# A decay-delta recurrence with a conv-gate MoE: the state spread to a block diagonal by GpSimd, wide products, and a new order

## The chip, the cores and the metric

The kernel runs on one core of one Trainium2 chip. Five engines work beside each other, each through its own instructions in program order: TensorE (PE; its weight loads are counted apart as PEld), VectorE (DVE), ScalarE (ACT), GpSimd (POOL) and SyncE (SP), which issues the DMAs. The metric is the device time of one execution in microseconds. The kernel before takes 618.69 us, the median of three runs between 618.66 and 619.24.

## What is computed

Per batch element and head a 40x40 state runs through 768 positions. Its decay works on the columns, and it is read by r and by a, and added to by outer products of v and k and of the read by a with b. What comes out is a token's 320 values, which pass through a matrix, a convolution of three positions, a gate and a second matrix.

```python
batch, n_heads, seq, head_dim = (4, 8, 768, 40)
...
for t in range(S):
    y[:, :, t] = np.einsum('bhd,bhde->bhe', rt, state)
    Sa = np.einsum('bhde,bhe->bhd', state, at)
    state_decay = state * wt[:, :, None, :] - np.einsum('bhd,bhe->bhde', Sa, bt)
    state = state_decay + np.einsum('bhd,bhe->bhde', vt, kt)
...
h = np.maximum(x @ w_in, 0.0)                 # 320 -> 1024
conv_out += conv_w[k][None, None, :] * hp[:, k:k + S, :]   # 3 positions
gate = 1.0 / (1.0 + np.exp(-conv_out))
return (h * gate @ w_out).astype(np.float32)  # 1024 -> 320
```

## The kernel before

**Tiles.** The sequence is cut into 24 steps of 32 positions (C), n = 0 to 23, and two steps make a pair j. Within a step the recurrence is solved in blocks: decays are brought to the step's ends as running products, so that the work of 32 positions becomes matrix products and one triangular solve per pair. The eight heads stand in three groups (NH = 3, 3, 2) of up to 120 rows, 3 heads by 40. The state `s` is a tile of [120, 4 batch elements, 3 groups, 40]: the rows are three heads under each other, each with its 40x40 block.

**A step, by names.** `wakb` loads w, a, k and b. `decays` (L474 to L496) makes the running products and `wc`, the decay over a whole step for each row, batch element and group. `decayed` makes `ah`, a times its decay, and the same for k and b. `scores` (L541 to L561) makes `ap`, a copy of `ah` for each head in which the rows of the two other heads of the group are zero (three activations with the column of `hmask` as scale, L547), and from it and k, b the scores `at`. The solve of a pair (L598 to L633) runs on GpSimd in 15 small steps, cut in pieces at 4, 8 and 12 (`CUTS`), except that of pair 0 on VectorE, and its result goes through DRAM (`xd`, `tt`, `nb`). `chain` (L637 to L733) is the recurrence itself, in stages: `pp` takes the product of the state with `ap` (L645, 32 matmuls with 120 rows, 32 columns of weights and 40 columns moving, one for each head and batch element) and adds that of the scores with v (L656); `pw`, `pe` and `pu` apply the solve (L668, L679, L692) with `psb` and `w` between them; `vu` gets the solved rows; `pn` is the update of the state (L711), which VectorE adds to the old state in four instructions (L726); and GpSimd multiplies the new state by `wc` in place (L732), so that the next step finds it decayed. Because `ap` is zero outside its head, a product over all 120 rows gives the head's own rows alone.

**Outputs.** `pvt` turns `vu` (L764), `pt` the decayed state into `sn` (L774, L776), `pm` are the scores of r (L523), `py` the step's output (L798, L809). Two steps make a window of 64 positions, which goes through the MoE: `ph` (L861), the gate `cc` on VectorE (L890), and `po` (L906). In the opening the weights are loaded and converted in pieces (`wi02` is a piece of the first matrix; its two parts are `wih` and `wil`), by ACT (L300), VectorE and GpSimd (L315, L342).

**What sets the order.** Each piece of work is a generator, advanced to its next `yield` by a token of a long string, `ORDER`; `ch3` advances the chain of step 3, `we5` the weights of piece 5, `dd2.0` the `decayed` of pair 2. `put` names for each stage the stages that have to be emitted ahead of it, mostly because of the number of buffers (`BUFS`). Each engine runs its instructions in the order in which the tokens emit them.

Of the kernel before, what the change touches and what calls it, by code (L numbers as in the profile page):

```python
# [40 lines left out]
    ha2 dd0.1 ch0 ut0*2 dd2.0 ch0 so1 ld2 we4 we6 we7 pa0 we7 ou0 we6 we8 ou0 ha3 rt0 ch1 ha3 ou0
    lv2 dd2.0 we6 dd2.0 so1 si1 dd2.1 we8 we7 ch1 ld2 so1 ch1 st1 we7 sc4 dd2.1 fi0 we9 lv2 dd2.1
    ch1 we9 fi0 ch1 sc4 so0 ut1 we9*2 ch1 ut1 si0 ld3 we7 ha3 ld3 ch1 we8*2 ou1 we10 we11 lr1*2 we10
    fi0 ch0 so1 de3.0 sc5 pa1 ch2 we10 sc5 we11 we10 ou0 we12 lv3 ou1 ch2 ha2 lv3 we12 st2 we11 ch2
    rt1 we10 ch2 ut1 we11 we13*2 we0 fi1 si2 so2 ch2 rt1 we13 fi1 we12*2 we14 we12 dd1.0 we9 fi1 lr2
    si2 pa0 de3.0 we11 de3.0 ld3 we8 dd2.0 we14 ch2 we14 ha4 we13 we15 ut2 ou2 ut2 ch2 so2 we14 so2
    we16 pa2 ha4 so2 de3.1 dd3.0 we15 ou2 we15*2 we5 we17 ut0 ro0 ch3 de3.1 lv1 ha5 fi2 ha4 st3 ch3
    we16 ch3 ha5 ch3 we17 pa0 ld3 pk0 we17*2 ld3 we16 ut2 we16 we18 lv4*2 st1 dd3.0*2 pk0 dd3.0
    dd3.1*2 fi2 we16 ro0 st2 ch3 we19 mi0.0 dd3.1 ut3*2 lr2 ou3 ld4 fi2 we17 we18 ch0 ch3 pa3 ch3
    sc6 we18 we17 fi1 sc6 sc7 mi0.0 sc7 we19 sc6 mi0.0 we18 ha5 so2 rt2 ou3 de0.1 ut3 we20*2 mi0.0  # L50
    we19*2 ch4 we17 mi0.0 we20 de4.0 ha6 we20 ch2 de3.1 mi0.1 we18 ch4 lv5 we21 mi0.0 mi0.1 rt2 ch4
    we21 mi0.0 lr0 mi0.1 rt2 ld4 ch4 we22 lv5 we21 st4 ut0 fi3 ha6 ch4 de4.0 we22 mi0.2 we18 ut4 fi3
    we19 fi3 de4.1 we19 ld4 we20 ch4 we19 ut4 ch2 ou4 ch4 si3 so3 pa4 mi0.0 mi0.1 mi0.2 lv5 mi0.2
    si3 ou4 de4.1 ld4 we21 ou3 mi0.3 mi0.1*2 dd4.0 ha7 st2 ld5 mi0.1*2 mi0.3 mi0.1 ch5*2 mi0.3 st5
    ha7 lr3 dd4.0 ch5 mi0.2 dd4.0 dd4.1 so3 lv6 we20 so3 mi0.1 mi0.2 ou4 we18 mi0.0 dd4.1 ch5 pk1
    mi1.0 sc8 pk1 ch5 ld5 mi0.3 mi0.0 mi0.2 ou5 so3 lr3 mi0.2 fi4 de5.0 dd4.1 ut5*2 mi0.2 ha6 mi0.3
    ch5 pa5 mi1.0 we20 so3 mi1.0 ha7 ch5 dd4.0 fi4 mi0.3 mi1.1 ou5 fi4 sc8 sc9 ch2 lr3 st6 lr3 mi0.3
    fi5*2 mi1.0 ch5 de5.0 lv6 dd5.0 lv7 lv6 rt3 pa2 ut2 ch6*2 rt3 lv7 mi0.3 mi1.1 lv6 fi4 mi1.1 lr4
    de5.0 mi1.2 lv5 fi5 ch6 lv1 sc9 ch6 mi1.1 mo0.0 ld5 mi1.0 rt3 mi1.1 ha8 lv8 ch6 ha8 mo0.0 lv7
    mi0.2 mi1.1 ut6*2 dd4.1 ou6 mi1.0*2 fi0 lv7 mi1.1 pa6 lr2 ch5 ch6 ou6 de2.0 fi3 mi1.0 mi1.1  # L60
    mi0.3 mo0.0 mi1.0 mo0.0 ha9 ha8 mi1.2 de5.1 lr4 ha9 ld5 mi0.3 si4 dd5.0 mi1.0 fi4 mi0.2 ld5 ch6
# [1086 lines left out]
```

## Time and profile before

| what | us |
|---|---|
| median of 3 runs | 618.69 |
| the profiled execution | 619.69 |
| its span, first to last instruction | 617.1 |
| the chain's products with the state, pp<-s,ap (L645) on PE | 19.2 busy |
| the state times its decay on POOL (L732) | 24.3 busy |
| the masked a, ap (L547) on ACT | 36.3 busy |
| weight loads of pp, one group of rows (L645) | 106 to 118 ns each |

The profile is of one execution. Busy time counts what an engine works on; several instructions of an engine may run beside each other on PE, where the four 32-column quarters of the array take separate products, so that PE's mean duration of one matmul is longer than the distance of their starts. In rows of matmuls, "120*32" is the rows and columns of the weights, "120x40" the rows and columns that move, and each matmul in these 32-bit numbers leaves two records. Releasers ("<-") are inferred.

### The profile page before, as it was taken

The numbers are of one execution on the slowest core, as the hardware profiler recorded it, in microseconds if no ns is written. First come the engines' busy times: TensorE is split into PE (matmuls) and PEld (weight loads), VectorE is DVE, ScalarE is ACT, GpSimd is POOL, SyncE is SP. The second block draws the span as 40 slices with busy tenths as digits, with TensorE's granted clock in tenths as the row PEclk, the third lists the DMA queues.
The fourth block names the chain that finished last, engine by engine and source line by source line (L and its number), as shares of the span: only waits on it lengthen the run. The fifth ranks groups of instructions, "written<-read, shape, count | busy, mean of one in ns | idle before, by whom it ended". The sixth has DMA issues, their size and how long they took to land.

```text
span 617.1 us, 32909 instructions
## 1 busy us (share of the span) xinstructions
PE 540.9 (88%) x14861; PEld 454.1 (74%) x14861; DVE 371.1 (60%) x757; ACT 349.2 (57%) x852; POOL 238.7 (39%) x573
## 2 busy tenths in 40 slices
PE   4465788879989999899899899889999899989998
PEld 3355667768868888778788788678787786877884
DVE  7887677778756645656467554447664473434560
ACT  2444455575765647656667466366765474555551
POOL 3414766625725435236145444045346054020100
PEclk9856987799999999999999999899999999899999
DMA  9966837375264561711735426424431302101001
GB/s 149 141 119 130 149 94 160 79 159 94 39 133 77 101 109 17 140 34 25 136 68 96 92 51 102 97 55 70 102 56 33 86 13 51 36 4 29 17 20 35
DMA packets 214767, 49.32 MB, mean 80 GB/s; under 512 B 203324, under 2 KB 208404, under 8 KB 214628
## 3 DMA queue, kind: packets, MB, share of 16 engines
q1 hardware_dynamic: 214628, 47.23, 40.3%
q8 instruction: 116, 1.90, 1.3%
q14 instruction: 23, 0.19, 0.1%
HBM read 36.72 MB, written 9.18 MB: 74 GB/s over the span
## 4 chain that ended last, share of the span: by engine, by line
PE 75%; DVE 7%; issue 6%; DMA 5%; ACT 5%; POOL 0%; SPq 0%; DVEq 0%; ACTq 0%
PE po L906 16%; PE ph L861 15%; PE pm L523 4%; PE ps L523 3%; PE pe L679 3%; PE pn L711 3%; PE pu L692 3%; PE pw L668 3%; PE py L809 3%; PE pp L656 3%; PE pvt L764 2%; PE pz L568 2%; PE py L798 2%; PE pp L645 2%; DMA xh<-xh 2%
## 5 line engine op out<-in xcount | busy, mean ns | idle before, releaser
L906 PE MATMUL po<-wo,g 128*128 128x320 f32 x384 | 117.4, 443 | 3.8 <-issue 3.8
L890 DVE SCALAR_TENSOR_TENSOR cc<-hb,cw,cc 128x256 f32<-128x256 f32 x192 | 95.9, 521 | 30.7 <-ACT cc L882 27.1
L906 PEld LDWEIGHTS po<-wo,g 128*128 128x128 f32 x384 | 69.2, 193 | 26.3 <-issue 4.8
L732 POOL TENSOR_TENSOR s<-s,wc 120x480 f32<-120x480 f32 x23 | 24.3, 1058 | 109.1 <-DVE s L726 89.4
L611 POOL TENSOR_TENSOR stg<-xx,bb 128x15 f32<-128x15 f32 (+4 forms) x165 | 54.9, 333 | 29.4 <-DMA bb<-bd 17.7
L617 POOL TENSOR_TENSOR xx<-xx,stg 128x15 f32<-128x15 f32 (+4 forms) x165 | 56.6, 343 | 12.9
L699 ACT COPY vu<-pu 32x320 f32<-32x320 f32 x96 | 40.0, 417 | 33.0 <-PE pu L692 31.2
L861 PE MATMUL ph<-xh,wih 120*128 120x256 f32 x288 | 56.8, 305 | 1.1 <-DMA xh<-xh 1.1
L726 DVE SCALAR_TENSOR_TENSOR s<-pn,side,s 120x240 f32<-120x240 f32 x90 | 35.9, 461 | 28.2 <-PE pn L711 28.2
L898 DVE TENSOR_TENSOR g<-cc,hb 128x512 f32<-128x512 f32 x48 | 36.5, 765 | 23.5 <-ACT cc L895 23.3
L837 POOL TENSOR_TENSOR xl<-xf,xh 120x384 fp32r<-120x384 f32 x24 | 25.4, 1057 | 59.6 <-ACT xh L835 59.6
L875 ACT ACTIVATE hb<-ph 128x512 f32<-128x512 f32 x48 | 28.6, 597 | 32.7 <-PE ph L861 28.9
L861 PEld LDWEIGHTS ph<-xh,wih 120*128 120x128 f32 x288 | 41.4, 192 | 4.7 <-DMA xh<-xh 1.5
L882 ACT ACTIVATE cc<-hb,cw 128x256 f32<-128x256 f32 x96 | 43.5, 507 | 0.0
L425 POOL COPY vu<-vin 96x240 f32<-96x240 f32 (+1 forms) x72 | 28.0, 425 | 37.0 <-DMA vin<-in_v_dram 24.7
L749 ACT ACTIVATE rp<-pr,hmask 120x384 f32<-120x384 f32 (+1 forms) x72 | 34.0, 551 | 12.3 <-PE pr L747 9.4
L683 DVE SCALAR_TENSOR_TENSOR psb<-pe,half,psb 128x320 f32<-128x320 f32 x24 | 13.2, 551 | 45.4 <-PE pe L679 44.9
L547 ACT ACTIVATE ap<-ah,hmask 120x384 f32<-120x384 f32 (+1 forms) x72 | 36.3, 573 | 7.0 <-DVE ah L502 6.9
L861 PE MATMUL ph<-xh,wil 120*128 120x256 f32 x192 | 38.9, 283 | 0.3
L523 PE MATMUL ps<-ap,kt 120*64 120x96 f32 (+1 forms) x576 | 31.0, 264 | 8.6 <-DVE wi01q L305 5.3
L861 PE MATMUL ph<-xl,wih 120*128 120x256 f32 x192 | 38.5, 282 | 0.0
L895 ACT ACTIVATE cc<-cc 128x512 f32<-128x512 f32 x48 | 30.2, 634 | 11.7 <-DVE cc L890 11.6
(306 smaller groups left out, 1179.2 us busy)
## 6 DMA issues: line engine op xcount, KB each, us to landing
inw<-in_w_dram SPq DMA_DIRECT2D x24, 160.0 KB
ina<-in_a_dram SPq DMA_DIRECT2D x24, 160.0 KB
ink<-in_k_dram SPq DMA_DIRECT2D x24, 160.0 KB
inb<-in_b_dram SPq DMA_DIRECT2D x24, 160.0 KB
vin<-in_v_dram SPq DMA_DIRECT2D x48, 80.0 KB
rin<-in_r_dram SPq DMA_DIRECT2D x24, 160.0 KB
out_dram<-ob SPq DMA_DIRECT2D x22, 160.0 KB
bd<-at SPq DMA_DIRECT2D x24, 128.0 KB
```

Source lines behind the costliest of these rows:

```text
L523: nc.tensor.matmul(ps[hs, y, pick(g), :], lhs(g, y)[:, hs], mk(pick(g), z, y), start=(g == 0 and y == 0), stop=True, skip_group_check=True,)
L547: nc.scalar.activation(out=ap[:, by_set(h)], in_=ah[:, : NH[h]], func=AF.Copy, scale=hmask[:, h : h + 1])
L611: eng.tensor_tensor(t3, xx[:, 0:nj, i : i + 1].to_broadcast([128, nj, nt]), bb[:, i : i + 1, i + 1 :].to_broadcast([128, nj, nt]), ALU.mult,)
L617: eng.tensor_tensor(xx[:, 0:nj, i + 1 :], xx[:, 0:nj, i + 1 :], t3, ALU.add)
L699: nc.scalar.copy(vu[q, y, :HD], pu[y][q])
L726: nc.vector.scalar_tensor_tensor(out=dst, in0=src, scalar=side[:, x : x + 1], in1=dst if x else old[:, zs], op0=ALU.mult, op1=ALU.add,)
L749: nc.scalar.activation(out=rp[:, by_rows(g), y], in_=pr[:GR, : NH[g]], func=AF.Copy, scale=hmask[:, g : g + 1],)
L861: nc.tensor.matmul(ph[:, j], l[:, fs], x, start=(j == 0 and i == 0), stop=(i == len(passes) - 1), skip_group_check=True,)
L882: nc.scalar.activation(out=cc[:, j], in_=hb[:, j, :, 1 : W + 1], func=AF.Copy, scale=cw[:, 1, f : f + 1],)
L890: nc.vector.scalar_tensor_tensor(out=cc[:, j], in0=hb[:, j, :, x : W + x], scalar=cw[:, x, f : f + 1], in1=cc[:, j], op0=ALU.mult, op1=ALU ...
L898: nc.vector.tensor_tensor(gt, cc, hb[:, :, :, 1 : W + 1], ALU.mult)
L906: nc.tensor.matmul(po[:rows, :DM], part(f), wo[:, f, :], start=(f == 0), stop=(f == NF - 1))
```

## The change

The first product of `chain` takes the unmasked `ah` as weights (32 columns: the positions), and what moves is no longer the state of one head but a tile `wide` (`se`, [120, 4, 3, 3, 40]): for each group, three blocks of 40 columns, the state with all rows but those of one head set to zero, a block diagonal. So one matmul with 120 columns covers three heads, one with 80 columns the two heads of the last group: 12 matmuls instead of 32. GpSimd makes `se` after the state's update, in three products of 120x480 with `ws`, ahead of the old product with `wc`, which stays for `pt` and the next update. `ws` is `wc` times `hmask`, made by GpSimd in `decays`, two small products a call. `ap` stays for the scores. `ah` now lives until the chain has used it, and has four buffers instead of two; `ap` has two instead of six, `ws` three and `se` one. `chain` takes `st["vu"]` a stage later. The string ORDER is another from its first line to its last.

```diff
--- before.py
+++ after.py
@@ -22,7 +22,7 @@
 VSOL = (0,)
 NWA = 24
 BUFS = dict(
-    rin=1, rs=1, vin=1, vu=2, hat=6, suf=2, pre=3, wc=3, at=3, ah=2, kt=1, ap=6, rp=1, bb=2, xx=2, stv=1, stg=1,
+    rin=1, rs=1, vin=1, vu=2, hat=6, suf=2, pre=3, wc=3, at=3, ah=4, kt=1, ap=2, ws=3, se=1, rp=1, bb=2, xx=2, stv=1, stg=1,
     tt=2, nb=2, s=2, psb=1, w1=1, vt=2, sn=2, g=6, ms=1, xf=1, xh=2, xl=2, hb=2, cc=2, o=2,
 )
 KINDS = dict(
@@ -33,116 +33,115 @@
 ORDER = """
-    ld0*2 de0.0*2 ld0 dd0.0 ld0 lv0 de0.1 we0 de0.1 dd0.0*3 de0.0 dd0.1*3 ld1 sc0 we1 ha0 we0 sc0
...
+    ld0*2 de0.0*2 ld0*3 de0.1 ld1 we0 lv0 dd0.0 de0.1 dd0.0*2 dd0.1*2 ha0 dd0.0 dd0.1 we1 sc0 lv0
...
 """
@@ -489,6 +488,18 @@
         al = pd["wc"].rearrange("p c (z y) g -> p y g z c", y=2)[:, y]
         nc.vector.tensor_tensor(al, ends(suf, 0), ends(wr, 1), ALU.mult)
         nc.vector.reciprocal(ends(dp0, 0), al)
+        if y == 0:
+            pd["ws"] = buf(wn, [GR, 2, B, G, 3], "ws", f"ws{j}")
+        nc.gpsimd.tensor_tensor(
+            pd["ws"].rearrange("p c (z y) g h -> p y c z g h", y=2)[:, y, 0],
+            pd["wc"].rearrange("p c (z y) g -> p y c z g", y=2)[:, y, 0].unsqueeze(3).to_broadcast([GR, 2, G, 3]),
+            hmask.unsqueeze(1).unsqueeze(1).to_broadcast([GR, 2, G, 3]), ALU.mult,
+        )
+        nc.gpsimd.tensor_tensor(
+            pd["ws"].rearrange("p c (z y) g h -> p y c z g h", y=2)[:, y, 1],
+            pd["wc"].rearrange("p c (z y) g -> p y c z g", y=2)[:, y, 1].unsqueeze(3).to_broadcast([GR, 2, G, 3]),
+            hmask.unsqueeze(1).unsqueeze(1).to_broadcast([GR, 2, G, 3]), ALU.mult,
+        )
         nc.vector.tensor_tensor_scan(
             out=flat(pd["pre"][:, y]), data0=flat(wr), data1=flat(dp0),
             initial=0.0, op0=ALU.mult, op1=ALU.add,
@@ -637,17 +648,19 @@
     def chain(st, nxt):
         n, c, pd = st["n"], st["c"], st["pd"]
         att = pd["at"]
-        first, old, vu = n == 0, state[n], st["vu"]
+        first, old = n == 0, state[n]
         pp = bank([128, HD], f"pp{n}")
         if not first:
-            for q, g, h in heads():
+            ah, wide = gbt(pd["ah"][:, c]), st["wide"]
+            for g in range(G):
                 for bi in range(B):
                     nc.tensor.matmul(
-                        pp[quad(bi), q * D : (q + 1) * D], st["ap"][:, q, quad(bi)],
-                        old[:, bi, g],
-                        start=(q == 0), stop=False, skip_group_check=True,
+                        pp[quad(bi), g * GR : g * GR + NH[g] * D], ah[:, g, quad(bi)],
+                        wide[:, bi, g, : NH[g]],
+                        start=(g == 0), stop=False, skip_group_check=True,
                     )
         yield
+        vu = st["vu"]
         for h in range(H):
             hc = slice(h * D, (h + 1) * D)
             for bi in range(B):
@@ -729,6 +742,14 @@
                     )
         yield
         w4 = nxt["pd"]["wc"][:, nxt["c"]].unsqueeze(3).to_broadcast([GR, B, G, D])
+        wide = nxt["wide"] = buf(wn, [GR, B, G, 3, D], "se", f"se{n}")
+        ws = nxt["pd"]["ws"][:, nxt["c"]].rearrange("p b g h -> p (b g) h")
+        for h in range(3):
+            nc.gpsimd.tensor_tensor(
+                wide.rearrange("p b g h d -> p (b g) h d")[:, :, h],
+                new.rearrange("p b g d -> p (b g) d"),
+                ws[:, :, h : h + 1].to_broadcast([GR, B * G, D]), ALU.mult,
+            )
         nc.gpsimd.tensor_tensor(new, new, w4, ALU.mult)
         yield

@@ -1018,7 +1039,7 @@
             put(
                 ("decayed", j, y), lambda pd=pd, y=y: decayed(pd, y),
                 (0, ("wakb", j), 2), (0, ("decays", j, y), 2), (0, ("decayed", j - 1 + y, 1 - y), 3),
-                (0, ("scores", 2 * (j - BUFS["ah"]) + 1), 1), (1, ("wakb", j), 3), (2, ("wakb", j), 4),
+                (0, ("chain", 2 * (j - BUFS["ah"]) + 1), 1), (1, ("wakb", j), 3), (2, ("wakb", j), 4),
                 (1, ("scores", n + 1 - 2 * BUFS["kt"]), 2), (1, ("hats", n + 1 - 2 * BUFS["kt"]), 2),
             )
         put(
@@ -1042,7 +1063,7 @@
         put(
             ("scores", n), lambda st=st: scores(st),
             (0, ("decayed", j, 1), 1), (0, ("scores", n - 1), 2), (1, ("decayed", j, 1), 3),
-            (1, ("chain", 2 * (j - BUFS["at"]) + 1), 2), (0, ("chain", n - BUFS["ap"]), 1),
+            (1, ("chain", 2 * (j - BUFS["at"]) + 1), 2), (0, ("scores", n - BUFS["ap"]), 2),
         )
         put(
             ("hats", n), lambda st=st: hats(st), (0, ("decayed", j, 1), 2), (1, ("decayed", j, 1), 3),
```

On PE, from the last matmul of step 10's state update (`pn101`) to the product of step 11 with the state (`pp11`). Before:

```order
L711 MATMUL pn101_5560<-vu0_142,hat101_4792 56x80
L764 MATMUL pvt101_5590<-ident_80,vu0_142 120x128 x3
L906 MATMUL po20_5535<-wo_154,g21_5157 128x320 x2
L798 MATMUL py10_5621<-sn10_5425,rp5_5339 32x40 x32
L523 MATMUL pm10_5655<-rp5_5339,vt100_5557 64x3x32 x2
L523 MATMUL pm10_5655<-rp5_5339,vt101_5594 64x3x32 x2
L523 MATMUL pm10_5655<-rp5_5339,vt100_5557 64x3x32 x2
L523 MATMUL pm10_5655<-rp5_5339,vt101_5594 64x3x32 x2
L523 MATMUL pm10_5655<-rp5_5339,vt100_5557 64x2x32 x2
L523 MATMUL pm10_5655<-rp5_5339,vt101_5594 64x2x32 x2
L645 MATMUL pp11_5671<-s10_5585,ap11_4304 32x40 x32
```

And now; `se10` is the spread state, and four matmuls of 80 columns follow the eight of 120:

```order
L785 MATMUL pvt100_5492<-ident_80,vu0_142 120x128 x3
L785 MATMUL pvt101_5498<-ident_80,vu0_142 120x128 x3
L927 MATMUL po20_5458<-wo_154,g21_4935 128x320 x2
L927 MATMUL po20_5458<-wo_154,g22_5311 128x320 x2
L534 MATMUL pm10_5508<-rp5_5202,vt100_5496 64x3x32 x2
L534 MATMUL pm10_5508<-rp5_5202,vt101_5502 64x3x32 x2
L534 MATMUL pm10_5508<-rp5_5202,vt100_5496 64x3x32 x2
L534 MATMUL pm10_5508<-rp5_5202,vt101_5502 64x3x32 x2
L534 MATMUL pm10_5508<-rp5_5202,vt100_5496 64x2x32 x2
L534 MATMUL pm10_5508<-rp5_5202,vt101_5502 64x2x32 x2
L819 MATMUL py10_5528<-sn10_5408,rp5_5202 32x40 x32
L657 MATMUL pp11_5564<-se10_5523,ah5_3431 32x120 x8
```

Between the two stand now both `pvt` and four matmuls of `po` instead of one `pvt` and two, and `py` has changed places with `pm`.

On POOL, in the solve of pair 1 (`xx1`, `stg1`) at the first state `s0`, before:

```order
L611 TENSOR_TENSOR stg1_3_710<-xx1_699,bb1_696 128x48
L617 TENSOR_TENSOR xx1_699<-xx1_699,stg1_3_710 128x4x12
L732 TENSOR_TENSOR s0_788<-s0_788,wc0_164 120x480
L611 TENSOR_TENSOR stg1_4_812<-xx1_699,bb1_696 128x55
L617 TENSOR_TENSOR xx1_699<-xx1_699,stg1_4_812 128x5x11
L611 TENSOR_TENSOR stg1_5_815<-xx1_699,bb1_696 128x60
```

And now, with a weight piece behind it:

```order
L622 TENSOR_TENSOR stg1_3_867<-xx1_856,bb1_651 128x48
L628 TENSOR_TENSOR xx1_856<-xx1_856,stg1_3_867 128x4x12
L748 TENSOR_TENSOR se0_885<-s0_773,ws0_175 120x12x40 x3
L753 TENSOR_TENSOR s0_773<-s0_773,wc0_164 120x480
L341 TENSOR_TENSOR wil_153<-wi11q_406,wih_152 120x256
L622 TENSOR_TENSOR stg1_4_943<-xx1_856,bb1_651 128x55
```

The spread of the state stands ahead of the product with `wc0`. Further on in the same solve, from its eighth step to its ninth, before:

```order
L611 TENSOR_TENSOR stg1_7_821<-xx1_699,bb1_696 128x64
L617 TENSOR_TENSOR xx1_699<-xx1_699,stg1_7_821 128x8x8
L315 TENSOR_TENSOR wi12q_828<-wi12q_828 120x256
L342 TENSOR_TENSOR wil_153<-wi02q_592,wih_152 120x256
L611 TENSOR_TENSOR stg1_8_948<-xx1_699,bb1_696 128x63
L617 TENSOR_TENSOR xx1_699<-xx1_699,stg1_8_948 128x9x7
```

And now:

```order
L622 TENSOR_TENSOR stg1_7_952<-xx1_856,bb1_651 128x64
L628 TENSOR_TENSOR xx1_856<-xx1_856,stg1_7_952 128x8x8
L314 TENSOR_TENSOR wi02q_939<-wi02q_939 120x256
L424 COPY vu0_142<-vin_136 96x2x120 x2
L424 COPY vu0_142<-vin_136 96x2x80
L341 TENSOR_TENSOR wil_153<-wi21q_587,wih_152 80x256
L314 TENSOR_TENSOR wi12q_972<-wi12q_972 120x256
L341 TENSOR_TENSOR wil_153<-wi02q_939,wih_152 120x256
L341 TENSOR_TENSOR wil_153<-wi12q_972,wih_152 120x256
L622 TENSOR_TENSOR stg1_8_1074<-xx1_856,bb1_651 128x63
L628 TENSOR_TENSOR xx1_856<-xx1_856,stg1_8_1074 128x9x7
```

The copies of v for step 2 (`vu0<-vin`) and more pieces of the first matrix (`wi`, `wil`) stand now inside the solve.

On ACT, around `w10`, the second stage of step 0's chain, before:

```order
L481 COPY wx0_148<-pw21_601 120x12x31
L482 COPY wx1_150<-pw21_601 120x12x31
L749 ACTIVATE rp0_434<-pr01_607,hmask_85 120x3x128 x2
L749 ACTIVATE rp0_434<-pr01_607,hmask_85 120x2x128
L300 ACTIVATE wi02q_592<-wi02r_591 120x256
L673 ACTIVATE w10_654<-pw0_621,half_105 128x320
L340 CAST wih_152<-wi21q_581 80x256
```

And now:

```order
L339 CAST wih_152<-wi01q_387 120x256
L480 COPY wx0_148<-pw20_565 120x12x31
L481 COPY wx1_150<-pw20_565 120x12x31
L686 ACTIVATE w10_624<-pw0_591,half_105 128x320
L581 COPY hat20_630<-pz20_626 128x360
L299 ACTIVATE wi21q_587<-wi21r_586 80x256
L480 COPY wx0_148<-pw21_654 120x12x31
```

`w10` stood behind the conversion of `wi02`; that conversion now comes sixteen instructions after it.

More of the change, by code (lines that the diff above doesn't have):

```diff
@@ L41 @@
[L41 to L61, printed above, removed]
@@ new lines @@
+    fi3 ch4 ha6 mi0.1 de3.0 mi0.2 we20 we22 ch4 fi3 ch4 mi0.1 st4 ut4*2 ou4 pa4 ou4 mi0.0 lv6 dd4.0
+    de4.1 ch5 so3 de4.1 so1 ch5 mi0.2*2 mi0.3 ha7 so3 ch5 mi0.1 pa4 ha7 dd4.0 mi0.1 ch5 st5 ld4 ha7
+    dd4.0 mi0.2 so3*2 st1 ld5 mi0.1 mi0.3 lr1 de4.0 mi0.2 si3 mi0.1 mi0.3 ch5 mi0.2 dd4.1 pk1
+    dd4.1*2 ut5 sc8 we21 fi4 mi0.2 ut5 de5.0 ch5 mi1.0 mi0.2 ou5 ld5 mi1.0 mi0.3 pa5 sc8 sc9 sc8 ou5
+    mi0.3 mi1.0 so3 mi0.3 ld5 mi0.2 lv6 lv7 mi1.0 lv6 lr3 rt3 ch5 mi1.0 ou5 mi0.1 mi1.1 lr3 mi0.2
+    ch6 mi1.0 ch6 ou1 fi4 mo0.0 fi4 fi5 fi4 mo0.0 rt3 lr4 mi1.0 mi0.3 dd2.1 de5.0 de5.1 ch5 lv6
@@ new lines @@
+    fi7 fi6 pk2 ld6 mi0.0 mo0.1 rt4 ch6 mi1.1 fi7 de6.0 de6.1 de6.0 st2 mi1.3 de5.0 mi1.1 ha10 fi7
+    rt3 mo0.1 mo1.0 ch8 ut7 fi6 mo0.1 sc11 ch8 mi1.3 mi2.0 mi1.2*2 mi2.0*2 we21 ch8 ro0 ha10 mi1.3
+    st8 mi2.0 mo0.1 de6.1 mi1.2 mi1.0 ch7 fi5 ch7 mi1.3 rt1 ch8 mi2.1 de4.1 mo0.1*2 ut6 mi2.1 ch8
+    mi1.0 lv9 lv7 mi1.2 ld7 mo1.0 lv1 ut8 mi1.3 ut8 dd6.0 mo0.0 mi2.1 si5 pa8 mi2.0 ou8*2 ha11*2
+    dd6.0 ch8 ou8 lr5 de7.0 dd6.0 de5.1 dd6.1 ch9 mi2.1*2 mi2.0 ha11 lv9 so5 lv9 ha11 mi2.0 mi1.2
+    lr6 dd6.1 ch9 mi2.0 st9 lv10 dd5.1 dd6.0 de6.1 ou8 dd6.1 pk2 mo1.0 lv8 mi1.3 mi2.1 ch9 mi2.2*2
@@ new lines @@
+    fi2 fi9 we22 mi3.1 mi1.3 si6 de7.0 ou7 mo1.1 so6 mi3.1 pk3 ld7 mi3.0 ou10 lv12 ha12 mi3.1 ch11
+    mi3.2 mi3.0 ld7 ch11 ch10 st11 mi3.1 mo1.0 mi2.3 ut5 so6 mo0.0 mi3.1 mi3.0 mo2.0 ha12 ha13*2
+    dd7.0 ha12 ha13 dd7.0 mo2.1 mi2.0 pa10 ch11 ld8 mi3.0 mi3.2*2 fi9 lv13 ch11 ch10 dd7.1 mi3.0
+    mi3.2*2 dd7.1*2 ch11 ut11 ut10 lv12 ut11 de8.0 so6 mi2.2 ou11 mo2.1 mi3.3 sc14 mi3.1*2 mi3.3
+    mi3.2 ha6 mi3.2 ch7 mi3.3 ch11 ch12*2 sc14 sc15 st3 mi3.3 pa11 mo2.1 pk4*2 ch11 fi10 ou11 ch11
+    mi3.1 ch10 ut11 fi10 lv13 mo2.0 ch12 ld8 fi10 fi11 de8.0 rt6 fi10 mi3.1 lr5 lv13 mi3.3 mi4.0
@@ new lines @@
+    ld11 dd11.1 st19 lv20 lr10 ch19 mi6.3 mi7.3*2 mi7.0 sc22 mi7.3 ch19 pa11 so10 lr1 fi15 ut19
+    dd11.1 mi7.2 rt8 mi7.2 ch19 lv21 fi18 st16 mi7.1*2 fi17 so2 so10 mi7.3 de11.1 pk8 ch18 mo5.0
+    mo6.0 ut19 mo6.1 lr11 mi7.2 sc22 pa19 mi7.3 ha21 ou19 ut18 ch20 sc23 rt10 mo6.0 sc23 ou19 ou18
+    fi18 dd11.0 ch19 mo6.1 ch20 lv18 mi7.2 mi7.3 st20 rt10 mo6.1 si11 mo6.1 ch20 mi8.0 fi18 mi7.2
+    ch20 ut19 mi7.3 mi8.0 mo6.1 mi8.0*2 pa18 lv21 lr11 fi16 mi8.0 pa6 mi8.1 mi7.3 st16 pa17 ch20
+    mi8.1 mi8.0 fi17 ha22 mi8.1 mo6.1 ch20 mi7.2 so11 sc23 rt10 st8 mi8.0 fi18 ut19 mi8.2 ou20 mo7.0
@@ new lines @@
+    mi8.3 mi9.1 st14 mi8.3*2 mi9.1*2 mo7.1 ch22 ch21 pa3 mi9.0 pa10 pa21 mi9.0 so11 ch22 mi7.2 ch18
+    mo8.0 st22 lv3 mo8.0 ch22 st22 ou21 mi9.0*2 lv2 mi9.2 mi9.0 fi20 mi9.2*2 ou21 rt11*2 ut7 mo8.0
+    mo8.1 ch22 mo8.0 ou22 mi9.1 lv23 mo8.0 st19 ch22 mi9.2 mi9.1 lv23 ch23 st9 mi9.1 ut22*2 mo8.1
+    fi21 pa22 mi9.2 mi9.1*2 ch23 fi20 dd11.1 mi9.0 mi9.1 st15 mi9.3 fi21 mi9.3 ou22 pk8 sc21 ou20
+    mi9.3*2 mi9.2 ut17 mi9.3*2 lv18 mo8.1 rt8 fi21 lr11 ch23 ha22 st23 mi9.3 mi9.1 pk10 mo8.1 si11
+    pk10 mi9.2 mo8.1 ha23 ch23 mi9.2 so7 mi10.0*2 mi9.2 mi10.0 st12 mi10.0 ch23 ha23 de9.0 mi9.3
@@ new lines @@
+    mi9.2 ch18 mi10.1 mi10.0 ut23 ch23 fi22 mi10.1 ou17 ut23 ou23 mi10.0*2 pa23 mi10.1 fi22 mi10.1
+    st21 mi10.1 mi10.0 mi10.2 mi10.1 mi10.2*2 mi10.3 ou23 mi10.2 mi10.1*3 mi10.3 st7 mi10.2 mo9.0
+    mi10.1 fi22 mi10.2 st17 mi10.3 mo8.1 mi10.0 mo9.0 ou22 fi23 mi10.3 fi22 mi10.3 mi10.0 fi23*2
+    pa23 mo9.0 mi9.3 lr1 mo9.0 fi23 pk11 mo9.0 rt10 mo9.0 st11 mo9.1*3 mi10.2 mo9.1*3 mi10.2*2
+    mi10.3 mi11.0 mi10.3 pa21 mi10.2 mi11.0*2 ou21 mi11.0 mi11.1 mi11.0 rt11 mi10.3 mi11.1 sc19 st23
+    mi11.1 lr1 mi11.0 st12 fi21 mi11.0 mi11.1 mi11.2 st21 mi11.1 mi11.0 mi11.2 mi11.1 pa14 mi11.2*2
```

160 lines of the change are left out of this document (72 added, 88 removed).

## The prediction

> **What bounds the kernel now.** I read the page's busy shares first, then the chain that ended last, then the busy time by stretches, then who waited for whom.
>
> ```profile
> span 617.1 us, 32909 instructions
> PE 540.9 (88%) x14861; PEld 454.1 (74%) x14861; DVE 371.1 (60%) x757; ACT 349.2 (57%) x852; POOL 238.7 (39%) x573
> PE 75%; DVE 7%; issue 6%; DMA 5%; ACT 5%; POOL 0%; SPq 0%; DVEq 0%; ACTq 0%
> ...
> 0.00:60.00 60.00, 30.32 (x466) 25.83 (x470) 47.94 (x118) 24.00 (x56) 19.31 (x62) 0.76 0.79 133
> 60.00:120.00 60.00, 47.65 (x1626) 40.32 (x1623) 43.32 (x97) 30.49 (x74) 42.54 (x97) 0.82 0.62 128
> 180.00:240.00 60.00, 57.86 (x1815) 48.63 (x1815) 34.01 (x65) 34.22 (x86) 28.76 (x74) 1.00 0.47 86
> ...
> PE pb L462 <- DMA inb<-in_b_dram: 10.1, 2, 9.0
> PE pe L679 <- ACT w L673: 5.7, 2, 5.5
> PE pp L656 <- issue: 5.5, 7, 1.8
> PE pp L645 <- issue: 1.8, 2, 1.6
> PE pm L523 <- DVE s L726: 0.3, 1, 0.3
> ```
>
> The third line is the chain by engine: TensorE (PE) makes 75% of it, GpSimd (POOL) nothing. In the stretches the columns are PE, weight loads, VectorE (DVE), ScalarE (ACT) and POOL. PE is busy half of the first 60 us, 47.65 of the next, and 57.86 of 60 from 180 on. From about 120 us on PE is the bound and what remains idle is mostly "issue", a stall with no visible cause (6% of the span, 37 us). Waits on data such as the 9.0 us for b, the 5.5 us for w and the VectorE wait of 0.3 us are rare, and the long ones lie in the opening. So a change of PE's work counts in full, and POOL's work counts only where it outgrows the PE work queued ahead of its reader.
>
> **The state product on PE.** Per step the 32 products of 120x32 with 40 columns become 8 with 120 columns and 4 with 80.
>
> ```profile
> L645 PE MATMUL pp<-s,ap 120*32 120x40 f32 x1472 | 19.2, 204 | 1.9 <-issue 1.8
> ...
> 346.38 1.08 PE po L906 x4
> ...
> 312.76 1.11 PE L523 MATMUL pm<-rp,vt 120*64 120x96 f32 x24
> 312.87 1.59 DVE L726 SCALAR_TENSOR_TENSOR s<-pn,side,s 120x240 f32<-120x240 f32 x4 [1.99 <-PE pn L711]
> 314.54 0.99 POOL L732 TENSOR_TENSOR s<-s,wc 120x480 f32<-120x480 f32 x1 [12.95 <-DVE s L726]
> 314.94 0.80 PE L798 MATMUL py<-sn,rp 120*32 120x40 f32 x64
> 315.61 0.68 PE L645 MATMUL pp<-s,ap 120*32 120x40 f32 x46
> ```
>
> Each matmul leaves two records: 1472 records are 23 steps of 64. The 64 of a step took about 0.68 us here (46 were kept), and 0.80 in the step of 273.56 quoted below; since missing records shorten a group, I take 0.77, nearer to the full one. What do 24 wide records take? The output rows of po cost 1.08 / 4 = 0.27 us for 320 columns, 0.84 ns each, so a record of 120 columns alone is 101 ns and of 80 columns 67 ns. An old record of 40 columns alone would be 34 ns, yet 64 in 0.77 is 12 ns each: the four quarters of the array (one for each batch element) run beside each other, and 64 x 34 / 4 = 0.54 of the 0.77 are columns, 0.23 something else. The wide ones have the same columns: 16 x 101 / 4 + 8 x 67 / 4 = 0.54. What may go is a part of the 0.23. If it goes with the number of records, 64 to 24, 0.14 goes; if it is a price per column or per group, nothing. I take 0.11, nearer to the first, as short records are where a start costs most. If they overlapped only in pairs, as pm's do (two halves of 64; 1.11 / 24 = 46 ns for up to 96 columns, 81 alone), it would be 1.08 + 0.11 = 1.19, a loss of 0.42. The better end is all of the 0.23 gone. Four quarters stand in both programs, so I take 23 x 0.11 = **2.5 us less**; the ends are 5 less and 10 more.
>
> [...]
>
> **Issue stalls.** PE's instructions fall by 20 matmuls, 40 records and 40 weight loads a step: 23 x 80 = 1840 of 2 x 14861, 6.2%. If the 37 us of issue stalls follow the instruction count, 2.3 us go; if they follow something else, none; twice that is the other end. I take **2.3 less**, the nearest row being the 1.8 and 5.5 us that pp's two groups alone lost to them.
>
> **Three new GpSimd products on the recurrence.** Between the end of the state update and the next step's pp, POOL now makes three copies `se` before its old product.
>
> ```profile
> L732 POOL TENSOR_TENSOR s<-s,wc 120x480 f32<-120x480 f32 x23 | 24.3, 1058 | 109.1 <-DVE s L726 89.4 <-PE pvt L764 19.6
> L732 POOL TENSOR_TENSOR s<-s,wc x23: 986/992/1367, 62.3 to 540.9; 120x480 f32<-120x480 f32 x23
> L611 POOL TENSOR_TENSOR stg<-xx,bb 128x15 f32<-128x15 f32 x22 | 5.6, 253 | 19.2 <-DMA bb<-bd 17.7
> ...
> 270.24 0.54 PE L764 MATMUL pvt<-ident,vu 128*120 128x128 f32 x3
> 271.86 2.66 DVE L890 SCALAR_TENSOR_TENSOR cc<-hb,cw,cc 128x256 f32<-128x256 f32 x4
> 272.02 1.16 POOL L732 TENSOR_TENSOR s<-s,wc 120x480 f32<-120x480 f32 x1 [0.36 <-DVE s L726]
> 273.56 0.80 PE L645 MATMUL pp<-s,ap 120*32 120x40 f32 x64
> ```
>
> A copy reads and writes what the old product does: 1.0 to 1.06 us each by the median and mean, 1.37 at the worst. 69 of them are 73 us; 48 small `ws` products at 0.25 add 12: POOL goes from 39% to about 52% busy. pp no longer waits for the old product, so the step from pn's end to pp is DVE's four (1.59 at 312.87) + three copies (3.0 to 3.2) + about 0.2 for two hand-overs, some 5.0 us, where it was 2.85 (312.76 to 315.61). pt, the turn of the decayed state for outputs, needs 6.0. PE must have that much other work there. In the new order, step 10 to 11 holds two pvt of 0.54, four po instructions (eight records of 0.27: 2.16), pm 1.11 and py 0.80: 5.15, just enough. Counted in the same rows, this gap of the new order holds 6 us or more in thirteen steps, 5.1 to 5.7 in six, and 4.1 to 4.6 in steps 1, 2, 3 and 5, where 0.4 to 0.9 is missing, 2.5 us in all, of which I count **0.5 more**, since those steps lie in the opening, where PE is not the bound. If the copies were all 1.37 (5.9 needed), the six would lack some 2.4 and the four 6: +8, the upper end; the lower is 0. What waits behind pp on PE is all of PE, so a miss costs in full. Behind the copies on POOL stand the old product and, in some steps, pieces of the triangular solve, whose result is due a pair later (below).
>
> [...]
>
> **The opening.** The new order also moves the weight conversions, and this changes two things before 100 us.
>
> ```profile
> 53.77 0.43 ACT L300 ACTIVATE wi02q<-wi02r 120x256 f32<-120x256 f32 x1 [1.76 <-DMA wi02r<-in_moe_w_in_dram]
> 54.11 0.51 ACT L673 ACTIVATE w<-pw,half 128x320 f32<-128x320 f32 x1
> 54.67 1.29 PE L679 MATMUL pe<-w,nb 32*32 32x40 f32 x64 [5.51 <-ACT w L673]
> 56.03 0.55 DVE L683 SCALAR_TENSOR_TENSOR psb<-pe,half,psb 128x320 f32<-128x320 f32 x1
> ...
> 67.92 0.73 POOL L342 TENSOR_TENSOR wil<-wi02q,wih 120x256 fp32r<-120x256 f32 x1
> ...
> 74.09 0.23 POOL L617 TENSOR_TENSOR xx<-xx,stg 128x15 f32<-128x15 f32 x1
> 74.34 1.31 SPq L623 DMA_DIRECT2D xd<-xx  x2
> 79.38 0.57 SPq L625 DMA_DIRECT2D tt<-xd  x1
> 88.57 1.00 PE L668 MATMUL pw<-psb,tt 32*32 32x40 f32 x48
> ```
>
> First, step 0: ACT's w stood behind the conversion of wi02, whose DMA was late, and PE waited 5.51 us for it. In the new order w stands ahead of that conversion. But the next in turn is psb on DVE (56.03), which there stands behind the a, k, b products and conversions of later pieces; so psb may start no sooner than before, and little of the 5.5 is gained: I take 2 (ends 0 and 5.5). Second, the solve of pair 1: its last product ended at 74.3, and the new order puts three copies (3.1) and one to four more conversions or loads' copies (0.73 each at 67.92) inside it, +4.0 to +6.5. The tt of this pair was issued at 79.38, lands 5 to 6 us later (estimate, from the 5.0 between the issues of xd and tt, which waits for it), and its reader pw started at 88.57: slack about 3. It is thus late by 1 to 3.5, at the worst 8; I take 2. The two cancel: **0**.
>
> **The other edits.** `ws` on POOL stands ahead of the step by a pair: hidden, 0 to +1. `ah` has 4 buffers and `ap` 2, so that scores wait for the scores before them rather than for the chain; both ends within 0.5, no row of the waits names ap or ah beyond 1.1 us. The last 70 us have the same shape in both orders: 0.
>
> **Sum.** -2.5 - 2.3 + 0.5 + 0 = -4.3 on the profiled execution, 619.7 us (span 617.1 and 2.6 around it): 615.4. The median of the runs shown is 618.7, 1.0 below, so **614.4**. Its own range is 609 to 617.4: down by the better ends of the state product (2.5) and the stalls (2.3) and a bit of the opening, up to where no change begins.
>
> **Rivals.** *POOL late in the opening* (22%, the slower side): the solve of pair 1 ends 6.5 us later, tt lands after 88.6 and pw with all PE work behind it slips by 6.5. It decides when the lateness exceeds the 3 us of slack. For it: POOL is 42.54 of 60 busy there, the fullest stretch. Against it: pw could start earlier only if step 0 does. Time: -2.5 - 2.3 + 0.5 + 6.5 = +2.2, or 621. *No change* (15%): issue stalls stay, since they may be tied to time and not to count, and the edge steps give back the 2.5: 618 to 619.5. *Wide products overlap only in pairs* (5%): 23 x 0.42 = +9.7 in place of -2.5, in all +7.9, or 626.6; pm speaks for it, the 12 ns against. [...]
>
> **How the numbers follow.** Forecast 56%, and the rivals 22, 15, 5 and 2%. A measurement of this kernel can tell about 0.2% (1.2 us) from no change. Faster 0.58 (forecast and floor), same 0.15, slower 0.27. The range from 608 to 624 takes in the forecast, no change and the late opening with 3 us around it, and leaves out 5 + 2% and the tails.
>
> **What would show it.** Right: pp from se as 24 records in 0.55 to 0.65 us; no PE wait on se above 0.5 us after 120 us; copies at 1.0 to 1.06; issue near 35 us; the PE stretch from 180 on still 57 of 60. Wrong: pp at 1 us or more; a row "pp waits for POOL se" of several us; tt of pair 1 landing after 88 us with pw waiting; or PE's own work shorter than I count, which would mean that the 40-column products cost more than their start-to-start shows.

## The result and the profile after

| set of runs | kernel before, median us | changed kernel, median us | ratio, 95% interval |
|---|---|---|---|
| first | 618.97 | 611.56 (609.3 to 613.0) | 0.9879 (0.9834 to 0.9923) |
| second | 612.17 | 612.05 (608.4 to 617.5) | 1.0014 (0.9975 to 1.0053) |
| fourth | 616.03 | 612.29 (607.5 to 616.3) | 0.9955 (0.9905 to 1.0005) |

The first set is the one that the prediction is measured by: 1.2% faster, 7.4 us. The medians are of all runs, while the ratios leave out those in a slower state of the chip (a fourth run of the kernel before took 639.2; the other three have the median 618.69 that is given ahead). Two later sets, on two different chips, ran the same two programs beside each other and give 0 and 0.5%; the third set had no changed kernel in it. The changed kernel stays at 612, the kernel before lies between 612 and 619 in the median. So the change is worth between nothing and 1.2%, and the 1.2 us that the prediction took for the resolution of a measurement is too fine: the kernel before alone moves by more than 6 us from set to set. What follows compares traces, where the parts are much larger than the whole.

From the page of the changed kernel (profiled at 613.0 us), with the queue that brings instructions; the row of the kernel before for that queue stands last:

```profile
span 611.3 us, 31181 instructions
PE 543.7 (89%) x13941; PEld 452.9 (74%) x13941; DVE 382.3 (63%) x757; ACT 349.3 (57%) x852; POOL 319.3 (52%) x690
PE 62%; POOL 11%; DMA 8%; DVE 6%; ACT 5%; issue 5%; SPq 2%; POOLq 0%; DVEq 0%; ACTq 0%
q8 instruction: 109, 1.79, 1.3%
```

```profile
q8 instruction: 116, 1.90, 1.3%
```

The chain that ended last now runs 11% of its time over POOL, where it had 0%. Matmuls and weight loads fall from 29,722 to 27,882, and the instruction packets from 116 to 109: one packet for 256.2 of them before and for 255.8 now.

Who PE waited for in the changed kernel (total us, times, longest):

```profile
PE pr L768 <- POOL rs L424: 6.6, 3, 4.9
PE pw L461 <- DMA inw<-in_w_dram: 5.6, 1, 5.6
PE ps L534 <- DVE wi01q L304: 4.9, 1, 4.9
PE pu L705 <- DVE psb L696: 4.5, 3, 2.3
PE pw L681 <- issue: 4.1, 3, 2.0
PE pp L657 <- POOL se L748: 4.1, 3, 1.5
PE py L830 <- issue: 3.9, 6, 1.2
PE pm L534 <- DVE s L739: 3.7, 1, 3.7
PE pp L669 <- issue: 3.2, 1, 3.2
PE pu L705 <- issue: 2.8, 3, 1.3
...
PE pe L692 <- ACT w L686: 2.2, 2, 1.4
```

Of the kernel before, the largest issue stalls beside those of pp, which the prediction shows:

```profile
PE py L809 <- issue: 5.9, 6, 1.7
PE pw L668 <- issue: 5.9, 6, 1.7
...
PE pe L679 <- issue: 5.6, 4, 1.6
...
PE po L906 <- issue: 3.8, 3, 1.7
```

Groups of the new work, from the view by line and shape:

```profile
L748 POOL TENSOR_TENSOR se<-s,ws 120x480 f32<-120x480 f32 x69 | 70.6, 1051 | 36.7 <-DVE s L739 33.3 <-PE pvt L785 3.0 <-PE po L927 0.4
L657 PE MATMUL pp<-se,ah 120*32 120x120 f32 x368 | 14.2, 272 | 4.1 <-POOL se L748 4.1
L657 PE MATMUL pp<-se,ah 120*32 120x80 f32 x184 | 7.5, 233 | 0.0
```

A copy takes 1.05 us. PE's busy time has not fallen (540.9 to 543.7) although pp with se now goes from its start to that of the next group in 0.69 us instead of 0.73 (medians of the 20 and 16 complete groups without a wait behind 120 us): busy time also holds half-clock stretches (32.4 us of granted clock are missing, 29.0 before) and each group's end (in the timeline a pp is busy for 0.76 us where the next group starts after 0.69; before, 0.80 and 0.73).

Summed over all rows of that view, issue stalls fall from 34.6 us (33 of them) to 16.7 (16), and all other waits of PE rise from 37.6 to 46.4. The state product gives 23 x 0.04 = 1.0. The share of granted clock that is missing, summed over stretches of 2 us, costs 32.4 us instead of 29.0. -17.9 + 8.8 - 1.0 + 3.4 = -6.7, and the span is 5.8 shorter. The terms overlap, since some of the missing clock lies inside waits, so this is a rough account. None of the four was foreseen in its size; the third came nearest (1.0 where 2.5 was taken). The 37 us of issue in the prediction are another count, the 6% of the chain that ended last; by that count 5% remain.

### The profile page after: what moved, and what is told of

Read it like the earlier page. It is cut to its first block, busy times and chain, and to the rows that moved or that the text cites. A ratio compares the mean times of both kernels' runs of the same rounds, so it can differ in the third digit from the quotient of the medians.

```text
span 611.3 us, 31181 instructions
## 1 busy us (share of the span) xinstructions
PE 543.7 (89%) x13941; PEld 452.9 (74%) x13941; DVE 382.3 (63%) x757; ACT 349.3 (57%) x852; POOL 319.3 (52%) x690
## 4 chain that ended last, share of the span: by engine, by line
PE 62%; POOL 11%; DMA 8%; DVE 6%; ACT 5%; issue 5%; SPq 2%; POOLq 0%; DVEq 0%; ACTq 0%
PE po L927 15%; PE ph L882 13%; PE ps L534 3%; PE pm L534 3%; POOL xx L628 3%; PE pn L724 3%; POOL stg L622 3%; POOL se L748 3%; ACT vu L712 2%; PE pu L705 2%; PE pvt L785 2%; PE py L830 2%; PE pz L579 2%; PE pp L669 2%; PE pw L681 2%
## 5 line engine op out<-in xcount | busy, mean ns | idle before, releaser
L911 DVE SCALAR_TENSOR_TENSOR cc<-hb,cw,cc 128x256 f32<-128x256 f32 x192 | 103.0, 558 | 33.3 <-ACT cc L903 29.9
L748 POOL TENSOR_TENSOR se<-s,ws 120x480 f32<-120x480 f32 x69 | 70.6, 1051 | 36.7 <-DVE s L739 33.3
L712 ACT COPY vu<-pu 32x320 f32<-32x320 f32 x96 | 40.1, 417 | 18.8 <-PE pu L705 16.7
L770 ACT ACTIVATE rp<-pr,hmask 120x384 f32<-120x384 f32 (+1 forms) x72 | 33.5, 544 | 18.0 <-PE pr L768 17.9
L493 POOL TENSOR_TENSOR ws<-wc,hmask 120x18 f32<-120x18 f32 x24 | 5.6, 234 | 58.3 <-DVE wc L489 57.8
```

The source lines that it names most:

```text
L712: nc.scalar.copy(vu[q, y, :HD], pu[y][q])
L748: nc.gpsimd.tensor_tensor(wide.rearrange("p b g h d -> p (b g) h d")[:, :, h], new.rearrange("p b g d -> p (b g) d"), ws[:, :, h : h + 1]. ...
L911: nc.vector.scalar_tensor_tensor(out=cc[:, j], in0=hb[:, j, :, x : W + x], scalar=cw[:, x, f : f + 1], in1=cc[:, j], op0=ALU.mult, op1=ALU ...
```

## The experiments

**Code and order taken apart.** The old and the new code under the old and the new order, and the new code with narrow matmuls, all in one set. The old code under the new order has four buffers each of `ah` and `ap`; the new code always has its own. In the last the 12 matmuls are cut into 32, on the same data and with the same waits:

```diff
-            for g in range(G):
+            for q, g, h in heads():
                 for bi in range(B):
                     nc.tensor.matmul(
-                        pp[quad(bi), g * GR : g * GR + NH[g] * D], ah[:, g, quad(bi)],
-                        wide[:, bi, g, : NH[g]],
+                        pp[quad(bi), q * D : (q + 1) * D], ah[:, g, quad(bi)],
+                        wide[:, bi, g, h],
```

> The changed kernel once more, as the measure for the runs beside it. Both theories: 0.988 of the kernel before, 609 to 613 us.

> The changed kernel with the product of ah and se cut into 32 matmuls of 40 columns instead of 12 of 120 and 80; same data, same waits, same order. Theory PE (the gain is that of fewer matmuls): the state product goes from 0.60 back to 0.75 us per step, 3.5 us, and the issue stalls from 17 back to 25 or 35 us: 619 to 626 us, no faster than the kernel before. Rival ORDER (the gain is the new order's, the wide product gives its columns' time and no more): 3.5 us at most, 612 to 615.

> The kernel before with the new ORDER string (ah 4, ap 4 buffers so that the rows come out in the new order, vu looked up a stage later), without se, ws and the wide product. Theory PE: the order alone gives little, 616 to 620 us. Rival ORDER: 608 to 613, and below the changed kernel if GpSimd's new work costs something.

> The changed code (wide product, three copies on GpSimd, new buffers) under the old ORDER string. Theory PE: the wide product gives its 3.5 us and about 10 of stalls here too, but the old order has only 2.2 to 3.1 us of PE work behind the state update in ten steps where 5 are needed, so some 2 us are lost in each: 618 to 630 us. Rival ORDER: with nothing gained by the code it is 630 or more.

| second set | median us | ratio to before, 95% interval |
|---|---|---|
| old code, old order (before) | 612.17 | 1 |
| old code, new order | 624.28 | 1.0252 (1.0196 to 1.0308) |
| new code, narrow matmuls, new order | 630.89 | 1.0344 (1.0299 to 1.0388) |
| new code, old order | 649.16 | 1.0647 (1.0607 to 1.0688) |
| new code, new order (the change) | 612.05 | 1.0014 (0.9975 to 1.0053) |

The ratio of 0.988 did not repeat. For the narrow matmuls and for the order alone the time lies outside the ranges of both theories. The 649 of the new code under the old order falls into the rival's "630 or more", but the rival's reason, that the order is the gain, is refuted by the 624. Neither the order nor the code is a gain by itself: the order alone costs 12 us, the code alone 37, and together they cost nothing. Under the new order the copies, with `ws` and the other buffers, cost 6.6 (624.3 to 630.9), and the wide matmuls give back 18.8 (630.9 to 612.05), of which their own pace is 1 (0.73 to 0.69 per step). Where the 18.8 is shows in the waits of the narrow version:

```profile
PE py L830 <- issue: 6.1, 4, 4.0
PE pp L669 <- issue: 5.7, 5, 2.4
...
PE pw L681 <- issue: 4.7, 3, 1.6
PE pe L692 <- issue: 4.3, 3, 1.9
```

Its issue stalls add up to 29.6 us, and the changed kernel's, in the trace of this set, to 12.5; the missing clock is 39.2 us instead of 34.1, and the other waits are 45.6 instead of 51.2. That makes 17.1 + 1.0 + 5.1 - 5.6 = 17.6, with the overlap said above, where the spans of these two traces differ by 15.2 and the medians by 18.8. Theory PE names the cause on this side, the issue stalls, though the time is above its range and the product's pace gives less than a third of what it said. Under the old order the new code waits on GpSimd:

```profile
PE pp L658 <- POOL se L749: 23.5, 15, 2.5
PE pw L682 <- ACT psb L675: 12.1, 4, 7.2
...
PE pt L796 <- POOL s L754: 9.6, 4, 5.6
```

The old order has less PE work behind the state update (ahead of step 11 the rows of the prediction make it 0.54 + 1.08 + 0.80 + 1.11 = 3.5 us, where 5 are needed), and 15 steps wait for se. Only 5.5 us of issue stalls are left there, beside 87.3 us of PE's other waits (with the copies made twice, below, 4.2 beside 95.0). In the changed kernel other waits are not the reason for fewer stalls, since the narrow version has as many other waits (45.6 us) and 29.6 us of stalls. Why the old code loses 12 us under the new order is open. Its only trace is of an execution of 634 us, and its issue stalls (33.1) are those of the kernel before; what differs is the granted clock, of which 42.7 us are missing instead of 29.0. In the five runs that its ratio is made of the clock is 0.938 to 0.953, in those of the kernel before in this set 0.950 to 0.964, which is some 8 of the 12 us (an estimate from the two means and the spans). What lowers the clock there is not shown.

**The kernel before once more.**

> The kernel before once more, for a trace beside these runs. If its time differs between the two sets of runs (618.7 in the first, 612 in the second) because of the chip, the trace shows fewer or shorter issue stalls, or a higher granted clock, than the 34.6 us and 0.953 of the first trace; if the first three runs were only a narrow draw, the trace is like the first and near 618.

It took 612.8 us, with the same granted clock (0.953) as in the first trace and 28.5 us of issue stalls instead of 34.6. That does not explain all of the 6.2 us by which its span is shorter: the other waits are 40.4 instead of 37.6, so waits differ by 3.3, and the rest is spread over PE's own work (538.3 busy instead of 540.9). In its set the kernel before ran from 610.6 to 624.5. I take it as scatter of this program and do not know its source.

**The copies' length.** Each copy made twice; the three in one instruction; and three copies by group of heads, where the last is shorter and pp's first matmuls need the first copy alone:

```diff
-        for h in range(3):
+        for h in (0, 1, 2, 0, 1, 2):
```

```diff
-        for h in range(3):
-            nc.gpsimd.tensor_tensor(
-                wide.rearrange("p b g h d -> p (b g) h d")[:, :, h],
-                new.rearrange("p b g d -> p (b g) d"),
-                ws[:, :, h : h + 1].to_broadcast([GR, B * G, D]), ALU.mult,
+        for g in range(G):
+            nc.gpsimd.tensor_tensor(
+                wide[:, :, g, : NH[g]],
+                new[:, :, g].unsqueeze(2).to_broadcast([GR, B, NH[g], D]),
+                ws[:, :, g, : NH[g]].unsqueeze(3).to_broadcast([GR, B, NH[g], D]), ALU.mult,
             )
```

> The changed kernel with each of the three copies made twice, +3.0 us of GpSimd between the state update and pp. Theory PATH (the copies are covered by the PE work placed there, but with little to spare): the gaps of the new order then lack 25 to 39 us in all, 637 to 651 us. Rival COVERED (GpSimd is idle 48% and the copies are hidden): under 5 us more, at most 617.

> The changed kernel with the three copies in one instruction of 120x1440. By the rows of 15 and 480 elements an instruction costs 0.19 us and 1.68 ns per element, so one takes 2.6 us instead of 3.0. Theory PATH: 0.4 us sooner in the steps that wait, 1 to 3 us less: 609 to 611. Rival COVERED: no difference, 612.

> The changed kernel with the three copies made by group of heads instead of by head: 480, 480 and 320 elements, so that pp's first four matmuls can start after the first copy, 2 us sooner, and the last copy is 0.3 us shorter. Theory PATH: 2 to 5 us less: 607 to 610. Rival COVERED: no difference, 612.

Twice: 669.67 us, ratio 1.0885 (1.0821 to 1.0949). One instruction: 608.79, 0.9895 (0.9835 to 0.9954). By group: 608.26, 0.9885 (0.9838 to 0.9932). The kernel before had 617.09 in this set. The times of the last two fit theory PATH, but without the changed kernel in the set they cannot be told from its 0.988 and 0.9955 elsewhere. The waits of the first:

```profile
PE pp L657 <- POOL se L748: 43.3, 17, 4.7
PE pt L795 <- POOL s L753: 7.5, 3, 2.8
```

PATH holds in kind, and the price was above its range (637 to 651): these two waits are 50.8 us, some 46 more, and the missing clock is 58.0 us, 26 more (a part of it lies inside the waits), while issue stalls fall to 4.2. The one instruction takes what the rows promised:

```profile
L747 POOL TENSOR_TENSOR se<-s,ws x23: 2607/2613/3050, 59.9 to 534.7; 120x1440 f32<-120x1440 f32 x23
```

**The better version beside the change.**

> The changed kernel beside the kernel before on one more chip: 0.988 in the first comparison, 1.001 in the second. A ratio between 0.985 and 1.005 is expected, and no statement about the sign from one set alone.

> The copies by group of heads, now beside the changed kernel in one set. Theory PATH: 3 to 5 us below the changed kernel of this set (0.5 to 0.8%). Rival COVERED, the copies' length does not matter and the earlier 0.9885 was the chip's: within 1.5 us of it.

In one set the changed kernel has 612.29, 0.9955 (0.9905 to 1.0005), and the copies by group 606.52, 0.9863 (0.9820 to 0.9907): 5.8 us or 0.9% less, a little above the 3 to 5 expected. The last copy takes 0.72 us instead of 1.0, and pp's waits for se fall from 2.5 us to 0.3 between the two traces of this set. That is less than half of the 5.8; the rest is not shown, since the traced executions happen to lie the other way round (610.0 by group, 607.5 for the changed kernel). By group is faster than the kernel before in both of its sets, which the changed kernel is not.

**The solve of pair 1 sooner.** On top of the copies by group, two pieces of the solve stand ahead of the weight conversions on GpSimd, by its tokens in ORDER:

```diff
-    de2.1 lv2 so1 we6 lv2
+    de2.1 lv2 so1*3 we6 lv2
...
-    we9 so1 ld3
+    we9 ld3
...
-    we6 so1 ch0
+    we6 ch0
...
-    rt0 lv3 ch1
+    rt0 lv3 so1 ch1
...
-    we11 so1 we9
+    we11 we9
```

> The copies by group, and the second half of pair 1's solve on GpSimd ahead of four weight pieces and the copies of v instead of behind them, with its DMAs ahead of the next load of k. The solve ends near 73 us instead of 81, tt lands near 84 and the wait of 4.35 us for it at pw of step 2 goes: 3 to 6 us below the run beside it. Rival: the next wait (w behind ACT's conversions, psb on VectorE, weight pieces that now come later) takes its place: within 1.5 us.

611.40, 0.9946 (0.9904 to 0.9988): 4.9 slower than without it, the rival's side and beyond. xd went out at 76.3 instead of 81.0, and no pw waited for tt. There was less to gain than the 4.35 us of the earlier trace: in the run beside it that wait was 1.4. In its place stands this, on ACT and then on PE:

```profile
74.52 0.40 ACT L342 CAST wih<-wi02q 120x256 fp32r<-120x256 f32 x1 [4.73 <-POOL wi02q L317]
74.83 0.52 ACT L689 ACTIVATE w<-pw,half 128x320 f32<-128x320 f32 x1
```

```profile
PE pe L695 <- ACT w L689: 9.0, 2, 8.4
```

ACT's w stands behind the conversion of wi02, which now waits for GpSimd. PE's waits for w are 9.0 us instead of 4.4 in the run beside it, about the difference of the two spans (612.7 and 608.3). It is the stall of the kernel before (5.5 us at pe) with another cause.

**What an issue stall depends on.** 456 short matmuls put PE's instruction count back, where instructions are sparse; they write columns that nobody reads:

```diff
+            if rows == 128 and f < NF - 1:
+                for i in range(3 if f < 6 else 1):
+                    nc.tensor.matmul(
+                        po[quad(i), 400:401], wo[:, f, quad(i)], wo[:, f, 0:1],
+                        start=False, stop=True, skip_group_check=True,
+                    )
```

> The changed kernel with 456 short matmuls (32 columns of weights, 1 column) added among the long ones of po, 19 per block, in columns of the bank that nobody reads. PE's instruction count is then again that of the kernel before, but the additional ones stand where PE's instructions are sparse. Theory DENSITY (issue stalls come where 250 instructions are used up faster than the next are brought): issue stalls stay at 12 to 20 us. Rival COUNT (stalls follow the number of instructions): 28 to 35 us. The time grows in both by the short matmuls' own pace, 4 to 10 us.

Issue stalls: 12.2 us, with 14,853 matmul records where the kernel before has 14,861 and 28.5 to 34.6 us. DENSITY, not COUNT. The own price of the short ones was misjudged by far: 662.43 us, 1.0773 (1.0710 to 1.0836). The timeline:

```profile
355.89 0.81 PE L927 MATMUL po<-wo,g 128*128 128x320 f32 x2
356.62 0.23 PE L932 MATMUL po<-wo 128*32 128x1 f32 x6
356.79 0.81 PE L927 MATMUL po<-wo,g 128*128 128x320 f32 x2
357.52 0.24 PE L932 MATMUL po<-wo 128*32 128x1 f32 x6
```

Two records of po and six of one column take 0.90 us, where two of po take 0.54 in a row (0.27 each): 0.36 for six columns, at 168 places (at 24 of them with two columns instead of six). The number of records alone does not make it, since 64 of 40 columns in a row take only 0.73, 11 ns each; what does is not shown.

## Why the prediction was right, point by point

**State product.** 0.11 us per step were taken, 0.04 measured, 1.0 in all instead of 2.5. The quarters do run beside each other (24 records of 272 and 233 ns in the mean take 0.69), so the direction was right; but most of the time beside the columns goes with the group, not with the number of records (beside the 0.54 estimated for the columns stand 0.19 with 64 records and 0.15 with 24), and 0.73 would have been the better start than 0.77. A floor per matmul, to which the chances give 2%, is shown by no run: the 64 records took 11 ns each, and the wide products gave 1.0 us in all.

**Issue stalls.** This is the term that was mis-sized: 2.3 (at most 4.6) against 17.9 (12 to 22 with the other traces of both kernels: 28.5 and 34.6 before, 12.5, 13.7 and 16.7 now). "Issue near 35 us", named as a sign of being right, failed. The prediction took the stalls to follow the number of instructions. Three things speak for bursts: the narrow version, whose 920 records in the dense place bring the stalls back; the short matmuls, whose 912 records do not; and the place of the stalls. In the first trace 127 matmul records stand between the stalls that begin at 86.25 and 89.58, 382 between those at 99.44 and 113.10, 128 between those at 482.08 and 485.49: near multiples of 128, as are all 32 distances of that trace (none is short of a multiple by more than 7). With a weight load each (14,861 of both kinds on the page), that is near multiples of 256, where the counts above give 256.2 matmuls and weight loads to a packet. The 128 records ahead of a stall took 3.3 us in the median, 128 records in a row anywhere 4.4. The 40-column products of a step are its densest stretch: 64 records in 0.72 to 0.73 us, 11 ns each (medians of complete groups without a wait behind 120 us), where one of po takes 0.27 us. In the changed kernel one such stall falls into the middle of a product, between two matmuls that need nothing new (first fence, PE's timeline; second, the stretches around it, where the last three columns are granted clock, DMA share and GB/s):

```profile
431.09 0.34 PE L669 MATMUL pp<-vu,at 32*32 32x40 f32 x16
434.68 1.02 PE L669 MATMUL pp<-vu,at 32*32 32x40 f32 x48 [3.25 <-issue]
```

```profile
428.00:431.00 3.00, 3.00 (x157) 2.35 (x155) 0.90 (x2) 1.81 (x5) 2.49 (x3) 1.00 0.15 55
431.00:434.00 3.00, 0.43 (x33) 0.28 (x21) 1.25 (x3) 0.64 (x2) 0.00 (x0) 0.90 0.57 137
434.00:435.00 1.00, 0.32 (x21) 0.32 (x24) 0.00 (x0) 0.00 (x0) 0.00 (x0) 0.50 0.23 55
435.00:437.00 2.00, 2.00 (x49) 1.91 (x40) 0.00 (x0) 0.44 (x1) 0.00 (x0) 0.50 0.23 59
```

That PE waits there for its next packet of instructions is shown by the packets' own times in the traces. Ahead of this stall one packet landed at 425.1 and the next, fetched from 432.2 on, at 433.1; PE went on at 434.68, 1.6 us later. All 33 issue stalls of the first trace end 1.2 to 1.6 us after a packet has landed, all 16 of the changed kernel's 1.3 to 1.7 us after one, and over all fourteen traces 244 of 248 end 1.1 to 1.7 us after one, but only 51 of PE's 376 other waits. Why a packet is fetched so late is not shown.

**The copies.** Their duration (1.05) and the 5 us from the update to pp held, and step 11, called just enough, is one of three that wait for se (the two others are steps 1 and 2, 1.26 us each; 3 and 5, called short too, do not wait):

```profile
275.98 0.76 PE L657 MATMUL pp<-se,ah 120*32 120x120 f32 x24 [1.53 <-POOL se L748]
```

But 0.5 us was too little: the three waits are 4.1 us, and the one above is over the 0.5 us that the prediction allowed behind 120 us. Of the copies the longest took 1.46. PE's waits behind 120 us, apart from issue stalls, rose from 3.3 to 10.2, of which 3.7 are one wait for VectorE's update and 1.5 this one for se. With fewer stalls PE may come sooner to everything else, so that waits that were hidden show; this is argued, and the narrow version, with its stalls back, has 45.6 us of other waits too. That the edge is steep, as the upper end of 8 said, is shown by the copies made twice, with some 46 us of waits more.

**The opening.** w is ahead as foreseen (PE's waits for it fall from 5.7 to 2.2), and psb on VectorE is next, as named (1.4 to 4.5). The solve of pair 1 ended late, as the first rival had it:

```profile
81.13 0.23 POOL L628 TENSOR_TENSOR xx<-xx,stg 128x15 f32<-128x15 f32 x1
```

```profile
81.39 1.33 SPq L634 DMA_DIRECT2D xd<-xx  x2
84.75 0.57 SPq L636 DMA_DIRECT2D tt<-xd  x1
```

That is 7.0 later than before. pw waited only 0.55 for it, at 89.74, since the slack of 3 us and PE's own delay took the rest. So that rival did not decide here. The 0 of this term was luck all the same, for the opening has larger changes that it did not list: PE's waits for the load of b fall from 10.1 to 1.2, and a new wait of pr for rs, which GpSimd makes, is 6.6. Ahead of 120 us PE's waits other than issue stalls add up to 34.3 us before and 36.2 now.

**The sum** was near by luck: a gain nearly eight times larger than thought met waits that were thought smaller and a loss of clock that was not in the sum. The direction of each listed part on PE was right, and the size of the largest was wrong. "No change", at 15%, is what the second set shows.

## What to carry to other kernels

Where PE is the bound and its stalls have no visible cause, look whether they end soon after an instruction packet has landed (1.1 to 1.7 us after one in 244 of 248 stalls here), and count the instructions in the dense stretches, not in the whole: fewer and wider matmuls there gave 18.8 us here, of which their own pace is 1. A longer path on another engine needs an order made for it, and an order made for it is no gain without it; change and order have to be measured together and apart. Short matmuls between full-array ones are not free: three of them, six records, cost 0.36 us here.
